# Two attention banks swapped, gh and gl moved into the visit, sines swapped, a third x2t buffer, and the first h of the fixed cycle in a bank of its own

## The chip, the cores and the metric

One core of a Trainium2 chip. The time is device microseconds of one launch, the median of several runs. Five engines run their own instruction queues in order: TensorE (PE), ScalarE (ACT), VectorE (DVE), GpSimd (POOL) and SyncE (SP, which issues the DMAs). PE writes to PSUM, eight banks of 128 x 512 fp32.

## What is computed

A linear attention with a complex decay per key dimension, and behind it two feed-forward layers:

```python
mag = np.sqrt(a_re * a_re + a_im * a_im)
scale = np.minimum(mag, 0.999) / (mag + 1e-06)
a_re_n, a_im_n = a_re * scale, a_im * scale
for t in range(S):                       # B, H, S, D = 4, 8, 768, 48
    new_re = ar * S_re - ai * S_im       # ar, ai: a_re_n, a_im_n at t, per (b, h, d)
    new_im = ar * S_im + ai * S_re
    S_re, S_im = new_re + kv, new_im     # kv = outer(k_t, v_t)
    y[:, :, t] = q_t @ S_re
x = y as 3072 tokens x 384
h = x @ w_in;  x = (h - tanh(h)) @ w_out     # layer 0, d_ff = 2048
h = x @ w_in2; x = relu(h)**2 @ w_out2       # layer 1
```

## The kernel before, in words

*Attention* is cut into 24 units: six chunks of 128 positions (c) for each of four batches (b), unit n = 4c + b. A unit takes logarithms and exponentials of the decay, sums them over positions on PE (pc: sums of the log magnitude; pu: sums of the angle), takes exponentials of pc (ee, in a7x) and two sines of pu's fractional part (fg, in a7 and a8; the last row of F goes by DMA to crow, for the same batch's next chunk), multiplies them into k and q (kn, qn), transposes these (pk, pq), forms masked products of k and q (strips, then wm on DVE), and from these and the state the outputs (px, to xh and xl); pU is the products of kn and v that are added to the state. Chunk 0 is written out in the string START; chunk c = 1 runs as not packed units, chunks 2 to 5 as packed ones.

*Feed-forward.* Six groups g of 512 tokens by 16 blocks m of the hidden width, twice (layers). For a block, g1 forms h in one bank (9 matmuls, because each operand is split into a high and a low float32r part), act_parts turns h into t, gh and gl (ACT: tanh, DVE: subtraction, ACT: the copy gh, DVE: gl = t - gh), and g2 adds to the three accumulators acc (9 matmuls). At a group's end of layer 0, put_x2 copies the three accumulators to tiles x2t (two buffers; ACT, DVE, ACT) and stores them by DMA to DRAM (x2d).

*The order of work.* block_step(t) issues block t's h, the activations of the block before, and the products acc of an older block. NB0 = 17 steps are layer 0's group 0. From t = 17 to 80 (NB0 <= t < NATT) the order is fixed: chain["on"] makes the class Turn issue every instruction of PE, ACT, DVE and SP behind the one traced before it on its engine. Outside of that a planner orders the instructions by its own costs. In the fixed cycle each unit's pieces lie at steps 0 to 15 of its own with a sort key within the step (the list at the end of `unit`: step, key, piece); units follow each other by four steps, so every fourth step is a *visit* (t - NB0 = 3 mod 4), in which one unit does its step 15 (strips, wm, pU, px), the next its 11, the one after that its 7 (a7x), and the next its 3 (a2). Keys below 5 come before the step's h, keys from 5 on after it. In a step, act_step(t, 1) twice does tanh with the subtraction, then gh, for the block just formed; act_step(t - 1, 3) at the next step's start does what is left, gl.

*Banks.* Until t = 17: three accumulators, two banks for h, three for attention. share_banks at t = 17 frees the latter five: two hold the strips (cleared by DVE), and three serve in turn as h, x and y. SHARED tells which of x and y a product uses. `late` is the unit's number past the first packed one; late 0, 1 and 2 straddle the step at t = 17.

*Tables.* ACT holds one table of functions at a time; `table` loads another where the next function isn't in it. tanh is in three of those used, exp and ln share one, sines need `silu_and_others`, arctan `sigmoid_and_others`.

Of the kernel before, what the change touches and what calls it, by code (L numbers as in the profile page):

```python
# [12 lines left out]
F32 = mybir.dt.float32  # L13
# [3 lines left out]
AF = mybir.ActivationFunctionType  # L17
ALU = mybir.AluOpType
AX = mybir.AxisListType
PSUM = bass.MemoryType.PSUM  # L20
# [4 lines left out]
TWO_PI = 6.283185  # L25
# [18 lines left out]
def kernel(  # L44
# [9 lines left out]
    nc = tc.nc  # L54
    B, S, HV, DP = v.shape
    H = HV * 2 // 3
    NG, DM, TG = out.shape
    D = DM // H
    P = 128
# [11 lines left out]
    fctx = ctx.enter_context(ExitStack())  # L71
    spool = fctx.enter_context(tc.tile_pool(name="spool", bufs=2))
    gpool = fctx.enter_context(tc.tile_pool(name="gpool", bufs=2))
# [4 lines left out]
    ps = {  # L78
        "c": ps_c,
        "h": pctx.enter_context(tc.tile_pool(name="ps_h", bufs=2, space=PSUM)),  # L80
        "a": pctx.enter_context(tc.tile_pool(name="ps_a", bufs=3, space=PSUM)),
    }
    SHARED = {"pU": "x", "px": "y", "pc": "x", "pu": "y", "pk": "x", "pq": "y"}
    strips = []

    def ps_tile(tag, name):
        if tag in ps:
            return ps[tag].tile([P, TG], F32, tag=tag, name=name)
        tag = SHARED.get(name, tag if tag in "hxy" else "x")
        return ps["shared"].tile([P, TG], F32, tag=f"s{tag}", name=name, bufs=1)  # L90

    def share_banks():
        pctx.close()
        del ps["h"], ps["a"]
        ps_s = fctx.enter_context(tc.tile_pool(name="ps_s", bufs=1, space=PSUM))
        ps["shared"] = fctx.enter_context(tc.tile_pool(name="ps_x", bufs=1, space=PSUM))
        for i in range(2):
            strips.append(ps_s.tile([P, HH, P], F32, name=f"strips{i}"))
            nc.vector.memset(strips[i], 0.0)

    x2g = [dpool.tile([KD, P, TG], F32, name=f"x2d{g}") for g in range(NG)]

# [9 lines left out]
    for g in range(4):  # L112
        m = maskab[32 * g:32 * g + 32, 1]
# [17 lines left out]
    b_hpi = const.tile([P, 1], F32, name="b_hpi")  # L131
# [5 lines left out]
    chain = {"on": False}  # L137
# [18 lines left out]
    ten, act_e, dve, sp = (Turn(e) for e in (nc.tensor, nc.scalar, nc.vector, nc.sync))  # L156
# [14 lines left out]
    def lut(*a, **kw):  # L171
        if general[0]:
            return act_e.activation(*a, **kw)
        with tc.issue_after(act_set["load"]):
            r = act_e.activation(*a, **kw)
        act_set["ops"].append(r.ins)
        return r
# [7 lines left out]
    n2 = 2 * DM  # L185
# [79 lines left out]
    def g1(layer, m, xt, h, cs=slice(0, TG)):  # L265
        wh, wl = wts[layer, m]
        xh, xl = xt
        n = 3 * KD
        i = 0
        for kk in range(KD):  # L270
            for w_, x_ in ((wh, xh), (wh, xl), (wl, xh)):
                ten.matmul(
                    h, w_[:, kk * P:(kk + 1) * P], x_[:, kk, cs],
                    start=(i == 0), stop=(i == n - 1),
                )
                i += 1
        return h
# [42 lines left out]
    def new_acc():  # L320
        return [ps_c.tile([P, TG], F32, tag="c", name="acc") for _ in range(KD)]

    def put_x2(acc, dst):
        for j in range(KD):
            t = gpool.tile([P, TG], F32, tag="x2t", name="x2t", bufs=2)
            if j % 2 == 0:
                act_e.copy(t, acc[j])
            else:
                dve.tensor_copy(t, acc[j])
            sp.dma_start(dst(j), t)  # L330
# [31 lines left out]
    xts = {}  # L362
# [9 lines left out]
    at = [xpool.tile([P, 2, HH, P], F32, tag=g, name=f"at_{g}") for g in ("xh", "xl")]  # L372
# [16 lines left out]
    def unit(n):  # L389
        c, b = divmod(n, B)  # L390
# [8 lines left out]
        tsl = slice(c * P, (c + 1) * P)  # L399
        HD = H * D  # L400
        V = {}
# [21 lines left out]
        packed = c >= 2  # L423
# [130 lines left out]
        def l3():  # L554
            if early_unit:
                V["vt"] = early("v")
                V["v"] = V["vt"].rearrange("p (h x) -> p h x", h=HV)
            else:
                V["v"] = vz
            sp.dma_start(V["v"], v[b, tsl])  # L560

        def a8():
            F, G = V["F"], V["G"]
            table("trig_and_small" if c == 0 else "silu_and_others")
            V["cs"] = V["ab"] if c == 0 else V["fg"]
            lut(V["cs"][:, :HD], F, AF.Sin, scale=TWO_PI)
            lut(V["cs"][:, HD:], G, AF.Sin, scale=-TWO_PI, bias=b_hpi)

        def a8x():
            dve.tensor_tensor(V["qk"], V["qk"], V["ee"], op=ALU.mult)  # L570
# [194 lines left out]
        if c == 0:  # L765
# [5 lines left out]
                px=a12, x=a12v, pU=a13, st=a13v, ff=fill,  # L771
            )
        def ready(name):
            if chain["on"]:
                table(name)

        if not packed:
# [9 lines left out]
                )  # L787
            ]
        late = n - 2 * B
        return [  # L790
            (0, 5.2, a0), (1, 5.2, a1), (3, 1.4, a2), (3, 1.5, lambda: ready("sigmoid_and_others")),
            (4, 5.1, a3), (5, 5.1, a3b), (6, 6.3 if late < 2 else 1.1, a6l),
            (6, 1.4, a0c), (7, 1.3, a7x), (7, 2.0, l2), (7, 6.1, a4), (7, 7.1, a5c),
            (8, 5.1, a7r), (9, 5.3, a5s), (9, 5.4, a8x),
            (10, 6.3 if late < 1 else 1.1, a6), (10, 6.4 if late < 1 else 1.2, a7),
            (10, 1.3, lambda: ready("silu_and_others")), (10, 6.5, a8),
# [8 lines left out]
    for n in range(B, NU):  # L805
        c, b = divmod(n, B)
# [4 lines left out]
    def attn(s, low=0, high=10):  # L811
        for key, f in sorted(plan.get(s, []), key=lambda x: x[0]):
            if low <= key < high:
                f()
# [170 lines left out]
    def x2_dst(g):  # L985
        return lambda j: x2g[g][j]
# [6 lines left out]
    NB0 = len(blocks)  # L993
# [4 lines left out]
    NB = len(blocks)  # L998
    NATT = NB0 + (NG - 2) * NM
    hs, gs = {}, {}  # L1000
# [8 lines left out]
    def second_half(n):  # L1009
        l, g, m, cs = blocks[n]  # L1010
        if m == 0 and cs.start == 0:
            cur["acc"] = new_acc()
        g2(l, m, gs.pop(n), cur["acc"], cs)
        if m == NM - 1:
            if l == 0:
                put_x2(cur["acc"], x2_dst(g))
            else:
                for j in range(KD):
                    put_out(cur["pool"], cur["acc"], g, j, vector=j % 2 == 1)
# [21 lines left out]
    def act_step(n, parts):  # L1041
        if n not in acts:
            acts[n] = act_parts(
                blocks[n][0], hs.pop(n), cur["pool"], lambda g: gs.__setitem__(n, g),
                third=NB0 <= n < NATT and n % 3 == 2,
            )
        for _ in range(parts):
            next(acts[n], None)

    def block_step(t):  # L1050
        steps = [t - NB0 + NM]
        chain["on"] = NB0 <= t < NATT
        if t < NB0:
            conv_upto(min(NM, blocks[t][2] + JOINS[t]))
            steps = ahead[t]
        if 0 < t <= NB:
            act_step(t - 1, 3)
        if t == NB0:
            share_banks()
        if t < NB:  # L1060
            l, g, m, cs = blocks[t]
            for s in steps[:-1]:
                attn(s)
            for s in steps[-1:]:
                attn(s, 0, 5)
            h = ps_tile("h" if t < NATT else "hxy"[t % 3], "h")[:, :cs.stop - cs.start]
            hs[t] = g1(l, m, xts[l, g], h, cs)
            for s in steps[-1:]:
                attn(s, 5, 6)
                if chain["on"]:  # L1070
                    act_step(t, 1)
                attn(s, 6, 7)
                if chain["on"]:
                    act_step(t, 1)
                attn(s, 7, 10)
        if t == NATT:
            actx.close()
            cur["pool"] = fctx.enter_context(tc.tile_pool(name="ap3", bufs=3))
            cpool[0] = cur["pool"]
        if t == NB:  # L1080
            finish()
            return
        while cur["g2"] < NB and cur["g2"] <= t - (LAG if t >= NATT + 2 else 2):
            second_half(cur["g2"])
            cur["g2"] += 1
        if t == NATT + LAG:
            conv_ahead()
        if t >= NATT + LAG:
            for _ in range(2):
                if cdone[0] < len(cq):  # L1090
                    conv_tick()
            m2 = cur["split"]
            if m2 in joined and t >= NATT + LAG + m2:
                conv_split(1, m2, joined.pop(m2))
                cur["split"] += 1
        if t >= NATT + 2 * NM and t % 2 == 0 and cur["recheck"] < 2 * NM:
            conv_check(*divmod(cur["recheck"], NM))
            cur["recheck"] += 1
        if t >= NATT + 2 * NM and t % 4 == 1 and cur["signs"] < NU // 2:
            sign_check(cur["signs"])  # L1100
            cur["signs"] += 1
        if t < NB and m == NM - 4:
            if l == 1 and g < NG - 1:
                xts[1, g + 1] = get_x2(cur["pool"], x2g[g + 1])
            if l == 0 and g == NG - 1:
                xts[1, 0] = get_x2(cur["pool"], x2g[0])
# [3 lines left out]
    first = {f"{n}{k}": f for n in range(B) for k, f in unit(n).items()}  # L1110
# [103 lines left out]
```

## Time and profile before

| | |
|---|---|
| median of 3 runs | 1036.53 us (1034.96 to 1038.94) |
| the profiled execution | 1038.07 us, of which the span from first to last instruction is 1035.9 |
| busy PE, ACT, DVE | 93%, 62%, 52% of the span |
| mean granted clock of PE | 0.981 of full speed |

All times below are microseconds from the span's start. Matmuls are pipelined: the next begins before the one ahead of it ends, so a row's duration is longer than the distance to the next row. A bracket at a row's end is the idle time of that engine just before it and whose end it waited for. Almost every instruction has the line of one helper (L150), so groups are told apart by the names of their tiles. A group with a count, as x45, is a run of like instructions.

### The profile page before, as it was taken

The numbers are of one execution on the slowest core, as the hardware profiler recorded it, in microseconds if no ns is written. First come the engines' busy times: TensorE is split into PE (matmuls) and PEld (weight loads), VectorE is DVE, ScalarE is ACT, GpSimd is POOL, SyncE is SP. The second block draws the span as 40 slices with busy tenths as digits, with TensorE's granted clock in tenths as the row PEclk, the third lists the DMA queues.
The fourth block names the chain that finished last, engine by engine and source line by source line (L and its number), as shares of the span: only waits on it lengthen the run. The fifth ranks groups of instructions, "written<-read, shape, count | busy, mean of one in ns | idle before, by whom it ended". The sixth has DMA issues, their size and how long they took to land.

```text
span 1035.9 us, 18373 instructions
## 1 busy us (share of the span) xinstructions
PE 965.9 (93%) x7424; PEld 797.5 (77%) x7424; DVE 543.8 (52%) x902; ACT 642.9 (62%) x1132; POOL 19.5 (2%) x41
## 2 busy tenths in 40 slices
PE   3999996998988998999999999999999999999997
PEld 1878775777777776777788887788888888888886
DVE  5899985565555655655654799322232322322211
ACT  8789877677566766776753445546656656555443
POOL 1000000000000000000000001000000000000000
PEclk9999999899989998999999999999999999999999
DMA  6535512222212222212113655005444344341000
GB/s 243 164 131 166 173 44 85 55 55 55 85 54 54 56 75 63 57 55 85 39 55 110 218 180 191 26 18 166 139 136 167 111 148 137 96 147 33 31 1 33
DMA packets 56946, 102.07 MB, mean 99 GB/s; under 512 B 23172, under 2 KB 32664, under 8 KB 56856
## 3 DMA queue, kind: packets, MB, share of 16 engines
q1 hardware_dynamic: 56712, 100.71, 30.5%
q8 instruction: 59, 0.97, 0.4%
q14 instruction: 31, 0.25, 0.1%
q10 hardware_dynamic: 144, 0.13, 0.0%
HBM read 88.14 MB, written 9.47 MB: 94 GB/s over the span
## 4 chain that ended last, share of the span: by engine, by line
PE 72%; ACT 12%; DVE 10%; DMA 4%; issue 1%; SPq 1%; POOL 0%; ACTq 0%; POOLq 0%; DVEq 0%
PE h L150 31%; PE acc L150 28%; PE px L150 4%; ACT L150 3%; DVE jw L150 3%; ACT fg L150 2%; DVE wl L150 2%; PE pU L150 2%; ACT ee L150 2%; DVE gl L150 1%; PE pk L150 1%; PE pq L150 1%; DMA x2d<-x2t 1%; PE strips L150 1%; ACT ab L150 1%; DVE t L150 1%
## 5 line engine op out<-in xcount | busy, mean ns | idle before, releaser
L150 DVE TENSOR_TENSOR gl<-t,gh 128x512 fp32r<-128x512 f32 (+1 forms) x193 | 132.6, 687 | 239.4 <-ACT gh L150 239.4
L150 ACT ACTIVATE t<-h 128x512 f32<-128x512 f32 (+1 forms) x193 | 114.8, 595 | 205.9 <-PE h L150 203.3
L150 PE MATMUL h<-xh,wh 128*128 128x512 f32 (+1 forms) x579 | 228.9, 395 | 8.3 <-DVE t L150 4.9
L150 PE MATMUL acc<-gh,wh 128*128 128x512 f32 (+1 forms) x579 | 228.5, 395 | 2.7 <-ACT x2t L150 2.7
L150 PE MATMUL h<-xl,wh 128*128 128x512 f32 (+1 forms) x579 | 226.0, 390 | 0.3 <-DVE xl L150 0.3
L150 PE MATMUL h<-xh,wl 128*128 128x512 f32 (+1 forms) x579 | 226.3, 391 | 0.0
L150 PE MATMUL acc<-gl,wh 128*128 128x512 f32 (+1 forms) x579 | 225.1, 389 | 0.0
L150 PE MATMUL acc<-gh,wl 128*128 128x512 f32 (+1 forms) x579 | 225.1, 389 | 0.0
L150 ACT CAST gh<-t 128x512 fp32r<-128x512 f32 (+1 forms) x193 | 119.2, 617 | 79.4 <-PE acc L150 38.6
L150 PEld LDWEIGHTS h<-xh,wh 128*128 128x128 f32 x579 | 108.9, 188 | 35.8 <-DVE t L150 7.5
L150 PEld LDWEIGHTS acc<-gh,wh 128*128 128x128 f32 x579 | 108.8, 188 | 24.8 <-ACT x2t L150 3.3
L150 PEld LDWEIGHTS h<-xh,wl 128*128 128x128 f32 x579 | 109.0, 188 | 22.9
L150 PEld LDWEIGHTS acc<-gh,wl 128*128 128x128 f32 x579 | 108.7, 188 | 22.6
L150 PEld LDWEIGHTS h<-xl,wh 128*128 128x128 f32 x579 | 109.0, 188 | 21.6 <-DVE xl L150 0.5
L150 PEld LDWEIGHTS acc<-gl,wh 128*128 128x128 f32 x579 | 108.9, 188 | 21.6 <-DVE gl L150 0.2
L150 DVE TENSOR_TENSOR t<-h,t 128x512 f32<-128x512 f32 (+1 forms) x97 | 66.1, 681 | 65.9 <-ACT t L150 65.8
L150 ACT ACT_TABLE_LOAD x66 | 84.7, 1283 | 1.9 <-PEq L1196 0.8
L150 ACT ACTIVATE t<-t 128x512 f32<-128x512 f32 x96 | 60.3, 628 | 1.7
L150 DVE TENSOR_TENSOR wmin<-wmin,cz 128x768 bf16<-128x768 bf16 x32 | 17.8, 557 | 57.4 <-ACT cz L150 57.4
L150 PE MATMUL pU<-vz,kn 128*32 128x48 f32 x816 | 17.1, 222 | 31.7 <-ACT ee L150 31.7
L150 PEld LDWEIGHTS pU<-vz,kn 128*32 128x32 f32 x816 | 15.1, 121 | 33.3 <-ACT ee L150 33.3
L150 DVE TENSOR_TENSOR wm<-strips,maskab 128x512 f32<-128x512 f32 x32 | 21.7, 689 | 33.2 <-PE strips L150 32.9
(125 smaller groups left out, 1025.7 us busy)
## 6 DMA issues: line engine op xcount, KB each, us to landing
st<-in_w_dram SPq DMA_DIRECT2D x32, 768.0 KB
sr<-in_w_dram SPq DMA_DIRECT2D x32, 768.0 KB
ri<-in_ri_dram SPq DMA_DIRECT2D x24, 384.0 KB
qk<-in_qk_dram SPq DMA_DIRECT2D x24, 384.0 KB
vz<-in_v_dram SPq DMA_DIRECT2D x21, 384.0 KB
x2d<-x2t SPq DMA_DIRECT2D x18, 256.0 KB
xf<-x2d SPq DMA_DIRECT2D x6, 768.0 KB
ss<-in_ri_dram SPq DMA_DIRECT2D x12, 384.0 KB
```

The source lines that it names most:

```text
L150: r = op(*a, **kw)
```

## The change

1. SHARED: pc goes to bank y and pu to bank x.
2. A pool "first" of one bank, made before the strips' pool, gives the h of the steps that ask for the tag "h" after share_banks; the strips and the shared banks lie behind it. The strips are cleared at the end of step 17 and not in share_banks.
3. put_x2 takes its third tile from the pool of the "cv" tiles while the fixed order is on.
4. Units of chunk 1 load 8 of the 12 head blocks that v holds (nv).
5. In packed units the sine with bias (on G) comes before the one on F.
6. For late 2, a2 moves one step earlier, for late 1, a7x one step earlier and a4 with a5c one step later.
7. In the step before a visit gh is no longer issued; in the visit gh follows the keys below 1.35 (the first strips with their mask product, and a7x), and gl follows the keys below 1.75 (a2, pU, the second strips with their mask product).
8. At t = 16 h and the first part of its activation are issued ahead of the attention pieces.

```diff
-    SHARED = {"pU": "x", "px": "y", "pc": "x", "pu": "y", "pk": "x", "pq": "y"}
+    SHARED = {"pU": "x", "px": "y", "pc": "y", "pu": "x", "pk": "x", "pq": "y"}
...
-        return ps["shared"].tile([P, TG], F32, tag=f"s{tag}", name=name, bufs=1)
+        pool = ps["first" if tag == "h" else "shared"]
+        return pool.tile([P, TG], F32, tag=f"s{tag}", name=name, bufs=1)
...
+        ps["first"] = fctx.enter_context(tc.tile_pool(name="ps_f", bufs=1, space=PSUM))
...
-            nc.vector.memset(strips[i], 0.0)
+
+    def clear_strips():
+        for z in strips:
+            dve.memset(z, 0.0)
...
-    def put_x2(acc, dst):
+    def put_x2(acc, dst, third=False):
         for j in range(KD):
-            t = gpool.tile([P, TG], F32, tag="x2t", name="x2t", bufs=2)
+            if third and j == 2:
+                t = spool.tile([P, n2], F32, tag="cv", name="x2t")[:, :TG]
+            else:
+                t = gpool.tile([P, TG], F32, tag="x2t", name="x2t", bufs=2)
...
-            sp.dma_start(V["v"], v[b, tsl])
+            nv = HV if packed else H
+            sp.dma_start(V["v"][:, :nv], v[b, tsl, :nv])
...
-            lut(V["cs"][:, :HD], F, AF.Sin, scale=TWO_PI)
-            lut(V["cs"][:, HD:], G, AF.Sin, scale=-TWO_PI, bias=b_hpi)
+            sins = [
+                lambda: lut(V["cs"][:, :HD], F, AF.Sin, scale=TWO_PI),
+                lambda: lut(V["cs"][:, HD:], G, AF.Sin, scale=-TWO_PI, bias=b_hpi),
+            ]
+            for f in sins[::-1] if packed else sins:
+                f()
...
+        ln = (2, 6.37) if late == 2 else (3, 1.4)
+        ex = (6, 6.36) if late == 1 else (7, 1.3)
+        at = (8, 6.05) if late == 1 else (7, 6.1)
...
-                put_x2(cur["acc"], x2_dst(g))
+                put_x2(cur["acc"], x2_dst(g), third=chain["on"])
...
-        if 0 < t <= NB:
+        visit = NB0 < t < NATT and (t - NB0) % 4 == 3
+        if 0 < t <= NB and not visit:
             act_step(t - 1, 3)
...
+            if t == NB0 - 1:
+                h = ps_tile("h", "h")
+                hs[t] = g1(l, m, xts[l, g], h, cs)
+                act_step(t, 1)
...
-                attn(s, 0, 5)
-            h = ps_tile("h" if t < NATT else "hxy"[t % 3], "h")[:, :cs.stop - cs.start]
-            hs[t] = g1(l, m, xts[l, g], h, cs)
+                attn(s, 0, 1.35)
+                if visit:
+                    act_step(t - 1, 1)
+                attn(s, 1.35, 1.75)
+                if visit:
+                    act_step(t - 1, 1)
+                attn(s, 1.75, 5)
+            if t != NB0 - 1:
+                h = ps_tile("h" if t < NATT else "hxy"[t % 3], "h")[:, :cs.stop - cs.start]
+                hs[t] = g1(l, m, xts[l, g], h, cs)
...
-                if chain["on"]:
+                if chain["on"] and (t - NB0) % 4 != 2:
                     act_step(t, 1)
                 attn(s, 7, 10)
+            if t == NB0:
+                clear_strips()
```

## Rows read from the trace of the kernel before

**Rows 1.** The page: busy time, share of the span and instructions of each engine.

```profile
PE 965.9 (93%) x7424; PEld 797.5 (77%) x7424; DVE 543.8 (52%) x902; ACT 642.9 (62%) x1132; POOL 19.5 (2%) x41
```

**Rows 2.** Sums of waits: who waited for whom, us in total, times, longest.

```profile
PE pU L150 <- ACT ee L150: 31.7, 12, 5.8
...
ACT x2t L150 <- DMA x2d<-x2t: 11.7, 5, 3.0
```

**Rows 3.** Timeline of an ordinary visit: start, duration, engine, operation, [idle before, releaser].

```profile
417.95 0.60 ACT L150 ACTIVATE fg<-fg,b_hpi 128x384 f32<-128x384 f32 x1
...
418.86 0.77 PE L150 MATMUL strips<-kqT 96*32 96x128 f32 x32
419.08 1.28 ACT L150 ACT_TABLE_LOAD   x1
...
420.38 0.87 ACT L150 ACTIVATE ee<-pc 128x384 f32<-128x384 f32 x2
...
421.30 0.84 PE L150 MATMUL pU<-vz,kn 128*32 128x48 f32 x45 [1.67 <-ACT ee L150]
...
422.55 1.06 PE L150 MATMUL px<-kqT,state 96*32 96x128 f32 x32
...
424.42 0.50 PE L150 MATMUL h<-xh,wh 128*128 128x512 f32 x1
...
427.44 0.69 DVE L150 TENSOR_TENSOR t<-h,t 128x512 f32<-128x512 f32 x1 [0.53 <-ACT t L150]
...
428.65 0.39 PE L150 MATMUL h<-xh,wh 128*128 128x512 f32 x1
```

**Rows 4.** Timeline of PE in the four long visits, the second of them whole.

```profile
183.62 1.42 PE L150 MATMUL pU<-vz,kn 128*32 128x48 f32 x45 [4.56 <-ACT ee L150]
...
282.17 0.77 PE L150 MATMUL strips<-kqT 96*32 96x128 f32 x32
288.75 1.42 PE L150 MATMUL pU<-vz,kn 128*32 128x48 f32 x45 [5.81 <-ACT ee L150]
...
294.25 0.50 PE L150 MATMUL h<-xh,wh 128*128 128x512 f32 x1
...
317.16 1.03 PE L150 MATMUL pU<-vz,kn 128*32 128x48 f32 x45 [3.50 <-ACT ee L150]
...
394.86 1.42 PE L150 MATMUL pU<-vz,kn 128*32 128x48 f32 x45 [4.98 <-ACT ee L150]
```

**Rows 5.** Windows: busy us by engine, then granted PEclk, DMA share, GB/s.

```profile
284.00:298.00 14.00, 9.25 (x160) 8.41 (x161) 6.26 (x13) 8.42 (x16) 0.00 (x0) 0.76 0.13 31
564.00:578.00 14.00, 14.00 (x63) 11.60 (x62) 8.10 (x11) 5.10 (x10) 2.21 (x3) 1.00 0.88 301
```

**Rows 6.** Timeline of ACT and of SP's queue (SPq) ahead of three long visits.

```profile
280.38 0.59 ACT L150 COPY x2t<-acc 128x512 f32<-128x512 f32 x1 [2.71 <-DMA x2d<-x2t]
...
309.74 0.57 SPq L150 DMA_DIRECT2D crow<-fg  x1
...
313.38 0.52 ACT L150 ACTIVATE fg<-fg 128x384 f32<-128x384 f32 x1 [1.83 <-DMA crow<-fg]
...
389.27 0.57 SPq L150 DMA_DIRECT2D crow<-fg  x1
...
391.09 0.52 ACT L150 ACTIVATE fg<-fg 128x384 f32<-128x384 f32 x1 [0.52 <-DMA crow<-fg]
```

**Rows 7.** Timeline of PE and ACT at the step that opens the cycle.

```profile
158.95 0.47 PE L150 MATMUL h<-xh,wh 128*128 128x512 f32 x1 [3.03 <-DVE state L150]
...
163.90 0.59 ACT L150 ACTIVATE t<-h 128x512 f32<-128x512 f32 x1
...
166.88 0.50 PE L150 MATMUL h<-xh,wh 128*128 128x512 f32 x1 [2.85 <-DVE t L150]
...
170.00 0.63 PE L150 MATMUL h<-xh,wl 128*128 128x512 f32 x1
```

**Rows 8.** Timeline of PE in the first visit of the last chunk.

```profile
495.42 1.45 PE L150 MATMUL px<-wm,vz 128*32 128x128 f32 x32 [1.79 <-DVE wm L150]
```

More of the change, by code (lines that the diff above doesn't have):

```diff
@@ L789, in unit @@
         late = n - 2 * B
+        ln = (2, 6.37) if late == 2 else (3, 1.4)
+        ex = (6, 6.36) if late == 1 else (7, 1.3)
+        at = (8, 6.05) if late == 1 else (7, 6.1)
         return [
-            (0, 5.2, a0), (1, 5.2, a1), (3, 1.4, a2), (3, 1.5, lambda: ready("sigmoid_and_others")),
+            (0, 5.2, a0), (1, 5.2, a1), ln + (a2,), (3, 1.5, lambda: ready("sigmoid_and_others")),
             (4, 5.1, a3), (5, 5.1, a3b), (6, 6.3 if late < 2 else 1.1, a6l),
-            (6, 1.4, a0c), (7, 1.3, a7x), (7, 2.0, l2), (7, 6.1, a4), (7, 7.1, a5c),
+            (6, 1.4, a0c), ex + (a7x,), (7, 2.0, l2), at + (a4,), (at[0], 7.1, a5c),
             (8, 5.1, a7r), (9, 5.3, a5s), (9, 5.4, a8x),
```

## The prediction

> **What bounds the kernel now.** I read the page first, then the sums of waits, then TensorE (PE), ScalarE (ACT), VectorE (DVE) and the SyncE queue (SP) in order of time, around each visit of the fixed cycle and around the step that opens it. PE is busy 93% of the span [rows 1], so a change can only pay where PE still stands idle or runs at its lower clock. The sums say where: twelve times, 31.7 us together, PE waits before the pU products for ACT's exponentials `ee` [rows 2]. ACT itself loses 11.7 us in five waits for an x2t buffer [rows 2].
>
> An ordinary visit shows why [rows 3]. The strips products start at 418.86. pU lies in bank x, and so does pc, from which ACT takes two exponentials. ACT runs sines, gh, table load, exponentials in that order; the exponentials end at 420.38 + 0.87 = 421.25, and pU starts at 421.30, after 1.67 us of idle PE. From strips to the visit's h are 424.42 - 418.86 = 5.56 us, so 3.89 without the wait.
>
> Twelve visits have this wait: eight ordinary ones and four long ones with 4.56, 5.81, 3.50 and 4.98 us, 18.85 together [rows 4]; the eight share 31.7 - 18.85 = 12.85, or 1.6 each. A long wait costs twice: after 5.81 us of idle the pU group took 1.42 us against 0.84, as the granted clock of 284 to 298, 0.76 on average, had part of it at 1.2 GHz and not 2.4 [rows 5], and from strips to h are 294.25 - 282.17 = 12.08 us: 3.89 of work, 5.81 of wait, 2.38 lost to the clock. Three of the long ones follow a group's end, where ACT stood 2.71 us before its second x2t copy; the fourth, at 317, follows a sine that stood 1.83 us for the crow transfer [rows 6].
>
> **The change part by part.** The sum is made on the profiled execution, 1038.07 us (span 1035.9 and 2.2 around it), 1.5 above the median of 1036.53.
>
> *pc and pu swap banks; gh and gl into the visit; ordinary visits.* pU then shares x with pu, whose readers are done a step earlier; px shares y with pc. PE: strips end at 421.30 - 1.67 = 419.63, pU starts at once, px follows 422.55 - 421.30 = 1.25 later, at 420.88, which is 2.02 after the strips' start. ACT: the sines end at 417.95 + 0.60 = 418.55; without gh there the load starts at once, so the exponentials end 1.28 + 0.02 + 0.87 = 2.17 later, at 420.72. px arrives about 0.1 after them. The 1.6 us go, and next in line is px behind the same exponentials with only that cover. I take 0.15 of new wait per visit, 1.45 gained, eight times 11.6; the bounds are 1.6 and 1.0 (exponentials 0.5 to 0.6 late, about the length of one sine). gh now stands on ACT between exponentials and logarithms, gl on DVE behind both mask products; their readers, the next step's acc products, come after that step's h. Behind them on DVE wait kn, qn, state, xl and the visit's subtraction, which frees the h bank: it ended at 428.13, the next h started at 428.65 [rows 3]. With PE 1.67 and DVE about 1.6 earlier that half microsecond stays; if it went, each visit would lose what is missing. No instruction is added.
>
> *Third x2t buffer, sines swapped; the four long visits.* With a buffer of its own the second ACT copy follows the first as soon as the accumulator is full, and 2.7 us of ACT's lateness go. The sine that reads G no longer stands behind the crow transfer, which reads F; the other one still does. What a crow transfer takes, from issue to the sine that waited for it, is 1.82 us in one place and 3.64 in another [rows 6]. For the visit at 282 I get: copy done 280.38 - 2.71 + 0.6 = 278.2, pu's reader and F, each 0.6 later, so crow issued 279.4, landed 281.2 to 283.0; sines done 281.8 to 283.5; exponentials 2.17 later, 284.0 to 285.7. px is ready at 282.17 + 2.02 = 284.19. It waits 0 to 1.5; I take 0.7, and 0.7 and 0.4 for its two sisters. At 317 the long transfer stays and the swap hides one sine of 0.5 and gh's move 0.6: sine 313.38 to 313.90, exponentials 316.07, px ready 314.91, wait 1.2. So the four keep 3.0 (bounds 1.2 to 5.7) of 18.85 + 8.4, where 8.4 is 2.38 for the clock at the first and 2.0 each for the others, an estimate by their pU rows (1.42, 1.42, 1.03 against 0.84). Gain 27.25 - 3.0 = 24.2.
>
> The three x2d stores now go out closer together, with crow behind them on SP's queue. The rows don't show that order mattering: crow took 1.82 us at a group's end (389.27) and 3.64 within a group (309.74) [rows 6]. The Trainium skill (DMA: Bandwidth & Descriptors, "Queues, rings and completion order") says that descriptors are consumed in ring order on each DMA engine, so crow would start behind the third store's 256 KB. By that rule the three waits lie at their upper ends, 2.5 us in all against my sum.
>
> The table load's price matters more: the load at 419.08 took 1.28 us, and the exponential began 0.02 after it [rows 3]. The Trainium skill (ScalarE: Activation LUTs, "What ACT_TABLE_LOAD costs") adds a drain of about 1.38 us to each switch. By it px would wait 1.3 us more in each of the 14 visits that have exponentials, some 18 us in all; the rows leave no room for such a drain.
>
> *Last chunk.* Its visits have no pU. At 495 px waited 1.79 us for a mask product [rows 8], held behind gl and gh after a late x2t copy: now about 0.65, gain 1.1. The next visit loses 0.5, since px comes there pU's 0.64 us sooner and meets the exponentials. The last two have none. Together 0.6.
>
> *h in an idle bank, and the three moved pieces.* At 158.95 the first h of the cycle starts after 3.03 us, behind state's read of the pU that lay in its bank [rows 7]. In the new bank it can start at 155.9. 18 products take 428.65 - 424.42 = 4.2 us [rows 3], transposes about 0.6: the second h could start at 160.7 and not at 166.88. What holds it is ACT: before the tanh at 163.90 lie sines, a table load, exponentials, logarithms, a second load, an arctangent and another tanh [rows 7]. The change puts the earlier tanh, exponentials and logarithms ahead of the sines, the arctangent and its load behind this tanh; that takes about 2.4 us (1.28 + 0.53 + 0.58) from in front of it, the subtraction and kn, qn still to come: second h at about 162.9, 4.0 gained. The eight starts from 166.88 to 170.00 took 3.12 us where 8 x 0.235 = 1.9 is usual, so 1.2 of lower clock go too. I take 5.2, bounds 0 (sines and so kn and qn now late) and 7.4. The er transfer goes out a step earlier, ahead of its reader; the strips are cleared a step's end later, three steps before their use.
>
> *v load.* A third less for the units before chunk 2. No PE wait above 1 us in those steps is on it: 0, at most 0.5.
>
> Sum: 11.6 + 24.2 + 0.6 + 5.2 = 41.6 us. 1038.07 - 41.6 = 996.5; on the median 1036.53 - 41.6 = 995. Bounds: 12.85 + 26.0 + 1.1 + 7.4 = 47 at the top (989), 8 + 21.5 + 0 + 0 = 29.5 at the bottom (1007). After the cycle nothing absorbs this: from 564 on PE is busy 14.00 of 14 us at full clock [rows 5], so a shift there shifts the end.
>
> **The rivals.**
> 1. The wait moves to px. For it: both stand behind the same exponentials, and the cover is 0.1 us. Against: px comes 1.25 us later than pU did, and gh leaves ACT ahead of them. With 1 us of wait in the 14 visits the gain is 41.6 - 12 = 30: 1007.
> 2. The opening step gains nothing, or loses 3 us. For it: outside the cycle the planner orders the instructions, and sines, kn and qn now stand behind more table work. Against: ACT had idle time there. 1000 to 1003.
> 3. The clock and the long waits stay: the x2t wait wasn't what made ACT late, or crow lands late again. Then the three visits keep 4 us each: 1007.
> 4. Slower: ACT becomes the loop's bound. px waits for exponentials, xh for px, the next tanh for xh, and the next exponentials for all of it. It decides from where the exponentials end 41.6 / 14 = 3.0 us later than worked out, about 4.9 after the strips' start; at 4 us later the time is 1036.5 + 14 = 1051. Against: in the cycle's other steps ACT stands waiting for h, so lateness doesn't add up.
> 5. The swap does nothing, because the planner's tile release still ties pU to an earlier reader: only x2t and sines (about 2.7 us of wait and 1 of clock in three visits), the last chunk and the opening step gain, 17 us: 1020.
>
> **How the numbers follow.** Chances: forecast 0.64, rival 1 0.12, rival 2 0.10, rival 3 0.05, rival 4 0.04, rival 5 0.05. Forecast 995; its own range 988 to 1001; with rivals 1 to 3 the range is 985 to 1010, leaving out rivals 4 and 5 and a little at both ends. A change within 0.5% (5 us) can't be told from none here. Faster than that: 0.94, the forecast and rivals 1, 2, 3 and 5 but for the outer 0.02 of their tails; within: 0.02; slower: 0.04, rival 4.
>
> **What would show it.** Right: no wait of pU for `ee`; px after strips by 2.0 to 2.3 us in ordinary visits; the way from strips to h under 4.2 us where it was 5.56; no x2t wait inside the cycle; the granted clock at full in the long visits; no wait of the first h for state. Wrong: a px wait for `ee` above 0.5 us in most visits, waits of h for the subtraction, or pk waiting for kn in the opening step.

## The result, and the profile after

The changed kernel takes 998.63 us, the median of four runs (995.56 to 1000.25); the kernel before took 1035.74 on the same chip. The ratio is 0.9636 [0.96, 0.9672]: 3.6% faster, with 995 forecast. The profiled execution is the fastest of the four, 995.56 (span 993.6, clock 0.996), against 1038.07 (span 1035.9, clock 0.981); the sum gave 996.5 for it. So the spans differ by 42.3 us and the medians by 37.1.

The page's line of busy time, after. PE is busy 12.8 us less with the same 7424 products [rows 1], as fewer of them run at the lower clock: px of the fifth visit takes 1.92 us in experiment 3, behind a long wait, and 1.08 here.

```profile
PE 953.1 (96%) x7424; PEld 786.6 (79%) x7424; DVE 543.4 (55%) x902; ACT 643.6 (65%) x1133; POOL 19.3 (2%) x41
```

The sums of waits, after: us in total, times, longest. The 31.7 us of pU behind `ee` [rows 2] are gone as a line; px waits for `ee` in six places, 4.5 us together (0.97, 0.87, 1.01 and 0.69 in the four long visits, 0.47 in each of two visits of the last chunk).

```profile
PE px L155 <- ACT ee L155: 4.5, 6, 1.0
PE pu L155 <- ACT kqT L155: 2.6, 1, 2.6
PE acc L155 <- ACT x2t L155: 2.5, 1, 2.5
...
ACT fg L155 <- DMA crow<-fg: 4.7, 5, 1.1
ACT x2t L155 <- DMA x2d<-x2t: 3.8, 2, 2.6
```

An ordinary visit after, PE and then ACT (start, duration, engine, line, operation). It answers to [rows 3].

```profile
383.48 0.77 PE L155 MATMUL strips<-kqT 96*32 96x128 f32 x32
384.06 0.81 PE L155 MATMUL pU<-vz,kn 128*32 128x48 f32 x45
...
385.30 1.06 PE L155 MATMUL px<-kqT,state 96*32 96x128 f32 x32
...
387.17 0.50 PE L155 MATMUL h<-xh,wh 128*128 128x512 f32 x1
```

```profile
382.04 0.61 ACT L155 ACTIVATE fg<-fg,b_hpi 128x384 f32<-128x384 f32 x1
382.55 0.51 ACT L155 ACTIVATE fg<-fg 128x384 f32<-128x384 f32 x1
383.07 1.28 ACT L155 ACT_TABLE_LOAD   x1
384.36 0.87 ACT L155 ACTIVATE ee<-pc 128x384 f32<-128x384 f32 x2
385.12 0.62 ACT L155 CAST gh<-t 128x512 fp32r<-128x512 f32 x1
```

No PE row has a bracket: no idle time. Strips to h is 387.17 - 383.48 = 3.69 us, where it was 5.56. The exponentials end at 384.36 + 0.87 = 385.23 and px, 1.24 behind pU, starts at 385.30: the cover of 0.1 us that the prediction worked out is about 0.07 here, and it holds. gh follows the exponentials on ACT.

The long visit that answers to the one at 282 [rows 4], PE, then ACT and SP's queue (SPq):

```profile
268.47 0.77 PE L155 MATMUL strips<-kqT 96*32 96x128 f32 x32
...
271.33 1.08 PE L155 MATMUL px<-kqT,state 96*32 96x128 f32 x32 [0.87 <-ACT ee L155]
...
273.22 0.50 PE L155 MATMUL h<-xh,wh 128*128 128x512 f32 x1
```

```profile
263.39 1.07 ACT L155 COPY x2t<-acc 128x512 f32<-128x512 f32 x2
...
268.57 0.52 ACT L155 ACTIVATE fg<-fg 128x384 f32<-128x384 f32 x1 [0.94 <-DMA crow<-fg]
...
270.41 0.87 ACT L155 ACTIVATE ee<-pc 128x384 f32<-128x384 f32 x2
```

```profile
266.14 0.57 SPq L155 DMA_DIRECT2D crow<-fg  x1
```

Both x2t copies now run as one group (x2) with nothing ahead of the second; what is left is the sine behind the crow transfer, and 0.87 us of px. Strips to h is 4.75 us where it was 12.08.

The step that opens the cycle [rows 7], PE, then ACT and SP's queue:

```profile
153.30 0.88 PE L155 MATMUL pU<-vz,kn 128*32 128x48 f32 x48
...
155.33 0.49 PE L155 MATMUL h<-xh,wh 128*128 128x512 f32 x1 [1.15 <-ACT xh L155]
...
161.64 0.39 PE L155 MATMUL h<-xh,wh 128*128 128x512 f32 x1
...
169.19 0.69 PE L155 MATMUL pu<-th,tri 128*128 128x384 f32 x1 [2.63 <-ACT kqT L155]
...
175.79 0.77 PE L155 MATMUL strips<-kqT 96*32 96x128 f32 x32
```

```profile
167.03 0.84 ACT L155 ACTIVATE ab<-ri 128x768 f32<-128x768 f32 x1 [4.70 <-DMA ri<-in_ri_dram]
```

```profile
162.87 0.43 SPq L155 DMA_DIRECT2D ri<-in_ri_dram  x1
```

The second h stands at 161.64 and not at 166.88. ACT then waits 4.70 us, until 167.03, for the load of `ri`, which SP issues only at 162.87, and PE waits 2.63 us for the kqT copies that stand behind it on ACT.

Windows of the long visit and of that place: length, busy us by engine (PE, PEld, DVE, ACT, POOL), granted clock, DMA share, GB/s. The long visit has the full 2.4 GHz (0.76 before [rows 5]); behind the ri wait part of the time is at 1.2.

```profile
268.00:282.00 14.00, 13.13 (x220) 10.97 (x219) 9.27 (x17) 10.81 (x20) 0.00 (x0) 1.00 0.31 88
169.00:176.00 7.00, 6.81 (x33) 5.42 (x37) 4.31 (x7) 4.98 (x9) 0.00 (x0) 0.76 0.38 128
```

**Where the 42.2 us came from**, from the start of the strips in the sixteenth visit, 558.13 before and 515.97 after; from there to the end it is 477.8 and 477.6 us. Strips to h is summed over the visits of a kind.

| part | before | after | gained | worked out |
|---|---|---|---|---|
| eight ordinary visits | 46.12 | 31.57 | 14.55 | 11.6 |
| four long visits | 42.71 | 19.06 | 23.65 | 24.2 |
| last chunk, its two visits with exponentials | 8.39 | 7.39 | 1.0 | 0.6 |
| opening step, pU of unit 7 to the first strips | 23.26 | 22.49 | 0.8 | 5.2 |
| up to that pU (start of it) | 155.03 | 153.30 | 1.7 | 0 |
| between visits, the rest | | | 0.5 | 0 |

### The profile page after: what moved, and what is told of

It is laid out like the page before. It is cut to its first block, busy times and chain, and to the rows that moved or that the text cites. A ratio compares the mean times of both kernels' runs of the same rounds, so it can differ in the third digit from the quotient of the medians.

```text
span 993.6 us, 18356 instructions
## 1 busy us (share of the span) xinstructions
PE 953.1 (96%) x7424; PEld 786.6 (79%) x7424; DVE 543.4 (55%) x902; ACT 643.6 (65%) x1133; POOL 19.3 (2%) x41
## 4 chain that ended last, share of the span: by engine, by line
PE 71%; ACT 10%; issue 7%; DVE 7%; DMA 4%; SPq 1%; POOL 0%; ACTq 0%; POOLq 0%; DVEq 0%
PE h L155 31%; PE acc L155 30%; PE px L155 4%; ACT L155 3%; ACT ab L155 2%; DMA crow<-fg 1%; PE strips L155 1%; ACT ee L155 1%; PE pk L155 1%; ACT fg L155 1%; PE pq L155 1%; DMA ri<-in_ri_dram 1%; DVE cv L155 1%; PE pU L155 1%; ACT gh L155 1%
## 5 line engine op out<-in xcount | busy, mean ns | idle before, releaser
L155 ACT ACTIVATE ab<-ri 128x768 f32<-128x768 f32 x24 | 20.3, 848 | 17.7 <-DVE ll L155 9.8
L155 DVE SCALAR_TENSOR_TENSOR jw<-st,jw 128x768 int32<-128x768 int32 x32 | 30.4, 951 | 0.2
```

The lines of the kernel that those rows point to most:

```text
L155: r = op(*a, **kw)
```

## The experiments

Each was timed in five rounds beside the kernel before. Experiments 8 to 11 ran on one chip and the other experiments on another; the ratio is to the kernel before on the same chip, so where two chips are compared the ratios count. A diff is against the changed kernel, except where it says before.

**1. Banks swapped back.**

```
-    SHARED = {"pU": "x", "px": "y", "pc": "y", "pu": "x", ...}
+    SHARED = {"pU": "x", "px": "y", "pc": "x", "pu": "y", ...}
```

> The changed kernel with pc and pu back in their old banks, all else kept. Theory: the bank swap is what lets pU pass the exponentials; without it pU waits again, by about 1.3 us in the eight ordinary visits (exponentials end 1.9 us after the strips start, pU is ready at 0.6) and 2.2 in the four with a late sine, less the px waits of 3.5 us that it replaces: +16 us, about 1014. Rival: moving gh off ACT ahead of the exponentials was what took the wait away; then no pU wait over 0.5 us and 999.

Measured: 1013.32 us, ratio 0.9766 [0.9744, 0.9788]. The wait is back in twelve visits (sums of waits, then PE's timeline in the ninth, the longest): 1.03 us in each ordinary one, 1.96 to 2.16 in the long ones. Strips to h in an ordinary visit is 4.92 us against 3.69. That it was the shared bank that held pU behind the exponentials is shown; the swap is worth some 14 us with the other edits in place (by the ratios, 13.5 against the first timing of the changed kernel and 14.7 against experiment 8).

```profile
PE pU L155 <- ACT ee L155: 16.4, 12, 2.2
```

```profile
374.21 0.84 PE L155 MATMUL pU<-vz,kn 128*32 128x48 f32 x45 [2.16 <-ACT ee L155]
```

**2. gh and gl back in the chain's step.**

```
-        visit = NB0 < t < NATT and (t - NB0) % 4 == 3
+        visit = False
...
-                if chain["on"] and (t - NB0) % 4 != 2:
+                if chain["on"]:
```

> The changed kernel with gh and gl back at the end of the step before the visit and the visit's start. Theory: the cover of px is 0 to 0.1 us, so gh's 0.62 us ahead of the table load shows as a px wait of about 0.5 us in each of 14 visits: +7 us, about 1006. Rival: ACT has slack there and px waits for its mask product anyway: 999.

Measured: 1004.03 us, 0.9689 [0.9669, 0.9709]. All fourteen visits with exponentials have px waiting; an ordinary one of the later ones takes 4.21 us. So it is gh's and gl's move that keeps the thin cover. The sums, and one visit's px:

```profile
PE px L155 <- ACT ee L155: 9.1, 14, 1.3
```

```profile
387.31 1.08 PE L155 MATMUL px<-kqT,state 96*32 96x128 f32 x32 [0.33 <-ACT ee L155]
```

**3. No third x2t buffer.**

```
-                put_x2(cur["acc"], x2_dst(g), third=chain["on"])
+                put_x2(cur["acc"], x2_dst(g), third=False)
```

> The changed kernel with two x2t buffers as before. Theory: ACT is 2.5 us late again in the three visits after a group's end, px waits that much longer and PE's clock falls there: +8 to +11 us, about 1008. Rival: with pU no longer behind ACT and gh moved, most of the lateness is covered: under +3 us, 1001.

Measured: 1011.24 us, 0.9738 [0.9718, 0.9758], 12.6 above the changed kernel's 998.63, or 10.6 to 11.8 by the ratios: at the upper end of the 8 to 11 expected or over it. Four visits suffer and not three: the first, fifth, ninth and thirteenth take 6.05, 9.02, 7.57 and 7.89 us, where the changed kernel has 4.86, 4.75, 4.57 and 3.70. In the fifth, ACT and then PE:

```profile
268.61 0.59 ACT L155 COPY x2t<-acc 128x512 f32<-128x512 f32 x1 [2.71 <-DMA x2d<-x2t]
...
274.95 0.87 ACT L155 ACTIVATE ee<-pc 128x384 f32<-128x384 f32 x2
```

```profile
270.40 0.77 PE L155 MATMUL strips<-kqT 96*32 96x128 f32 x32
...
275.87 1.92 PE L155 MATMUL px<-kqT,state 96*32 96x128 f32 x32 [3.48 <-ACT ee L155]
```

The wait of 2.71 us is as long as that of [rows 6]. It moves through ACT's queue to px, and the px group then takes 1.92 us instead of 1.08.

**4. The swap alone, on the kernel before.**

```
-    SHARED = {"pU": "x", "px": "y", "pc": "x", "pu": "y", ...}
+    SHARED = {"pU": "x", "px": "y", "pc": "y", "pu": "x", ...}
```

> The kernel before with the bank swap alone. Theory: pU's wait goes, px waits for the exponentials that still stand behind gh, 0.55 us in ordinary visits; gain about 1.1 us in each of eight, 1.3 and about 1 of clock in each of four: -18 us, about 1018. Rival: the swap alone brings nearly all that the visits gained (-31): about 1005; other rival: it brings nothing, the wait moving to px whole: 1035.

Measured: 1024.93 us, 0.9878 [0.9859, 0.9896]: 13 us and not 18. The twelve visits with pU are not where it falls short. The eight ordinary ones take 4.2 to 4.3 us and gain 11.8 together. The long ones keep 7.83, 10.88, 6.16 and 8.27 us, their wait now before px, and gain 9.6, about what was expected. What the expectation left out is the rest. The first two visits of the last chunk, which had no pU to wait, now wait with px and take 7.56 and 4.21 us where they took 5.38 and 3.01; the ways between visits are 2.9 us longer in all; and from the sixteenth strips to the end it takes 480.3 us and not 477.8.

```profile
PE px L150 <- ACT ee L150: 22.4, 14, 5.3
```

**5. h of the opening step back in its old bank, the moved pieces kept.**

```
-        pool = ps["first" if tag == "h" else "shared"]
+        pool = ps["shared"]
...
-        ps["first"] = fctx.enter_context(...)
```

> The changed kernel with the first h of the cycle back in a bank that the attention used. Theory as predicted: h waits for state's read of pU again, 3.0 us; behind it ri's landing hides most, so 0 to +2 at the end, 999. Rival: with the moved pieces DVE does state right behind pU, 154.8, and h waits for xh until 155.3 anyway, so the bank is worth nothing here: no wait on state, 998.3.

Measured: 996.05 us, 0.9593 [0.9567, 0.9619], not slower than with the bank. The first h waits for its own operand `xl` and not for state; DVE reads pU for state at 153.70, as soon as pU is done. So with the moved pieces the bank is worth nothing that can be measured. PE, then DVE:

```profile
152.76 0.88 PE L154 MATMUL pU<-vz,kn 128*32 128x48 f32 x48
...
155.41 0.47 PE L154 MATMUL h<-xh,wh 128*128 128x512 f32 x1 [1.76 <-DVE xl L154]
```

```profile
153.70 0.55 DVE L154 TENSOR_TENSOR state<-state,pU 96x384 f32<-96x384 f32 x1 [0.44 <-PE pU L154]
```

**6. The moved pieces back, the bank kept.**

```
-        ln = (2, 6.37) if late == 2 else (3, 1.4)
+        ln = (3, 1.4)
...
-            if t == NB0 - 1:
+            if False:
...
```

(and `ex` and `at` in the same way, and the h of that step issued behind the attention work again.)

> The changed kernel with the opening step as before: a2, a7x and a4 at their old steps, h and its activation of step 16 not ahead of the attention pieces; the bank of h kept. Theory: the second h is late again by some 3 us, as the tanh ahead of it stands behind tables once more; but the changed kernel waits for ri a step later until about 167, so only 0 to 2 us of it reach the first visit: 998 to 1000. Rival: the moves are worth their whole 4 us: 1003.

Measured: 1000.16 us, 0.9639 [0.9614, 0.9664]; the interval holds the changed kernel's 0.9636. The second h of the cycle comes at 167.74 again, but no ri wait follows, and the strips start at 177.43. The first h of the cycle now waits longest of all, 7.47 us, and by its bracket for DVE's `t`, a subtraction that reads an earlier h, where the kernel before had 3.03 us for state [rows 7]. So the new bank by itself does not let the first h start early; it only exchanges one reader for another. From unit 7's pU, at 152.40 here, to the first strips it takes 25.03 us, more than the 23.26 of the kernel before.

```profile
160.75 0.79 PE L155 MATMUL h<-xh,wh 128*128 128x512 f32 x1 [7.47 <-DVE t L155]
```

**7. The whole v load again.**

```
-            nv = HV if packed else H
+            nv = HV
```

> The changed kernel with v loaded whole in the units before chunk 2. Theory: the 1.7 us by which pU of unit 7 starts sooner (155.0 before, 153.3 after) isn't the smaller load, as no PE wait there names it: 998.3. Rival: the 128 KB less per unit bring the queue's later loads forward: +1.5, 1000.

Measured: 998.89 us, 0.9623 [0.9597, 0.965], no difference. Its profiled execution, the slowest it had, has unit 7's pU 2.6 us later than the changed kernel's. The other profiles say the same: with the whole load that pU starts at 155.03 (before), 155.12 (experiment 4) and 155.88 (here), and in all eleven profiles with the smaller load at 152.40 to 154.53. So the 1.7 us in the table point to the smaller load, although the time of the kernel shows nothing of it; where it is lost again was not looked for.

```profile
155.88 0.88 PE L155 MATMUL pU<-vz,kn 128*32 128x48 f32 x48
```

**8. The changed kernel once more, unchanged.**

> The changed kernel again, on the same chip as the next three: 998.6 by its earlier median, 995.6 to 1000.3. If the visits with a px wait for the exponentials (1, 5, 6 and 9 of 16 in its first profile) are others this time, they are the visits where a crow transfer happened to be late; if they are the same, their place in the schedule makes them.

Measured: 998.22 us, 0.9624 [0.9596, 0.9651]. The px waits stand in the same visits, the four long ones and two of the last chunk, so they belong to the order of the work. What differs most between the two profiles is the change of layers at 607: there acc waits 3.48 us for an x2t copy, against 2.55 in the first profile, and PE's granted clock is 0.61 in that stretch where it was 1.00. From the sixteenth strips to the end it took 481.0 us, not 477.6. The changed kernel's timeline and window, then those of this run:

```profile
607.30 0.50 PE L155 MATMUL acc<-gh,wh 128*128 128x512 f32 x1 [2.55 <-ACT x2t L155]
```

```profile
606.00:612.00 6.00, 4.70 (x21) 3.89 (x22) 5.42 (x7) 3.66 (x7) 0.00 (x0) 1.00 0.15 58
```

```profile
608.67 0.80 PE L155 MATMUL acc<-gh,wh 128*128 128x512 f32 x1 [3.48 <-ACT x2t L155]
```

```profile
606.00:612.00 6.00, 3.33 (x8) 2.66 (x9) 4.22 (x6) 3.45 (x6) 0.00 (x0) 0.61 0.28 107
```

**9. F in a tile of its own**, so that no sine overwrites what the crow transfer still reads.

```
             if c > 0:
                 pair("fg", "F", "G")
+            if packed:
+                t1("F", F32)
```

> The changed kernel with F in a tile of its own in the packed units, so that the sine on F no longer overwrites what the crow transfer reads and waits for nothing. Theory: the px waits left over (0.7 to 1.0 us in four visits, 3.5 together) are crow's; without them -3.5 us, 995, and the px distance is 1.83 in all twelve visits with pU. Rival: ACT is late there by its own work; then the waits stay and the time is 998.6.

Measured: 992.9 us, 0.9566 [0.9536, 0.9595], 5.3 below experiment 8. ACT has no crow wait any more, and px comes 1.82 to 1.83 us behind the strips in every visit with pU but the first. The fifth, ACT and then PE:

```profile
266.88 0.51 ACT L155 ACTIVATE fg<-F 128x384 f32<-128x384 f32 x1
```

```profile
267.81 0.77 PE L155 MATMUL strips<-kqT 96*32 96x128 f32 x32
...
269.63 1.07 PE L155 MATMUL px<-kqT,state 96*32 96x128 f32 x32
```

The px waits alone were worked out at 3.5. The other part lies in the opening step, where the ri wait is gone as well: SP issues that load at 161.52 and no longer at 162.87, and ACT, which comes to it later, waits by its bracket for DVE instead. From unit 7's pU to the first strips it takes 20.53 us, against 22.91 in experiment 8. SP's queue, then ACT:

```profile
161.52 0.43 SPq L155 DMA_DIRECT2D ri<-in_ri_dram  x1
```

```profile
166.66 0.85 ACT L155 ACTIVATE ab<-ri 128x768 f32<-128x768 f32 x1 [1.11 <-DVE ll L155]
```

**10. Unit 11's ri load issued a step earlier.**

```
-            (0, 5.2, a0), ...
+            ((-1, 1.0) if late == 3 else (0, 5.2)) + (a0,), ...
```

> The changed kernel with unit 11's load of ri one step earlier, ahead of the opening step. Theory: the opening step gained only 0.8 us where 5.2 were worked out because, shorter, it meets that load: ACT's square waits 4.7 us for it, PE 2.6, and PE's clock falls behind it; without it -4 us, 994.6, and visit 1 starts about 13.5 us after the first h and not 20. Rival: something behind it on ACT or DVE is as late (qn, the table loads), so that under 1 us comes back: 998.

Measured: 997.2 us, 0.9615 [0.9588, 0.9643]: mostly the rival. The ri wait goes and the first strips start at 171.65, 4.1 us sooner; but now the exponentials of the first visit are late, px waits and runs at the lower clock, and h comes at 179.07, 7.42 after the strips instead of 4.86. 1.6 of the 4.1 us are left in the profiles; the medians, 1.0 us below experiment 8's with intervals that overlap, can't be told apart. ACT, then PE:

```profile
172.80 0.52 ACT L155 ACTIVATE fg<-fg 128x384 f32<-128x384 f32 x1 [0.99 <-DMA crow<-fg]
...
174.63 0.87 ACT L155 ACTIVATE ee<-pc 128x384 f32<-128x384 f32 x2
```

```profile
171.65 0.77 PE L155 MATMUL strips<-kqT 96*32 96x128 f32 x32
...
175.56 1.94 PE L155 MATMUL px<-kqT,state 96*32 96x128 f32 x32 [1.92 <-ACT ee L155]
```

**11. Experiments 9 and 10 together.** Both diffs above.

> Both edits together. Theory: they add, -7.5 us, about 991. Rival: each uncovers the other's successor, -4 us: 994.5.

Measured: 993.39 us, 0.958 [0.9548, 0.9612], no better than 9 alone. The rows of experiment 9 say why: there the ri wait is gone already, and from unit 7's pU to the first strips it takes 20.44 us here against 20.53 there.

**12. Both, and the third x2t buffer in every group**, so at the change of layers too.

```
-                put_x2(cur["acc"], x2_dst(g), third=chain["on"])
+                put_x2(cur["acc"], x2_dst(g), third=True)
```

> ri earlier, F in a tile of its own, and the third x2t buffer also outside the fixed order. Theory: the one x2t wait left, at the change of layers, costs PE 2.5 to 4.0 us and in some executions 1.5 to 4 more of lower clock behind it, which is most of the scatter between executions; without it about 988.5, executions within 3 us of each other. Rival: there the next wait (x of layer 1, or the weights on DVE) ends as late: 993, scatter as before.

Measured: 987.53 us, 0.952 [0.9493, 0.9546], the fastest of all kernels here, 11 us below the changed one and 5.9 below experiment 11 (6.2 by the ratios). The acc wait is gone, PE is busy without a gap there at full clock (window below), and the executions lie within 2.6 us of each other.

```profile
596.00:611.00 15.00, 15.00 (x68) 12.43 (x67) 8.64 (x12) 8.49 (x14) 0.00 (x0) 1.00 0.37 139
```

The swap of the sines was not undone by itself; experiment 9 takes away what it was for.

## Why the prediction was right, step by step

- *Ordinary visits* (11.6; measured 14.55). The mechanism is the one worked out, and experiments 1 and 2 show both halves of it. In the visit at 383 the size was low on two terms. The 0.15 us of new px wait didn't come: rival 1, with px behind the exponentials everywhere, is what experiment 2 gives, in a smaller size. And pU starts 384.06 - 383.48 = 0.58 after the strips and not 0.77, since a group that waits for nothing starts before the modelled end of the one ahead; a bracket of 1.67 us was worth 5.56 - 3.69 = 1.87. So px comes 1.82 us behind the strips, a little under the 2.0 to 2.3 that were to show the prediction right. But the eight are not alike, as the working took them to be. The last five gained 9.0 of the 14.55. The third visit kept 4.51 us and gained only 0.94; the fourth kept 4.47, and both stay over the 4.2 us named as a sign. The fourth still gained 2.72, as before it took 7.19 us: its 1.65 us of wait was followed by lower clock (the kernel before, window below), and that came back too. The working costed lower clock in the long visits alone.

```profile
256.00:264.00 8.00, 6.35 (x180) 5.70 (x179) 4.75 (x9) 6.11 (x11) 0.00 (x0) 0.79 0.02 4
```

- *Long visits* (24.2; 23.65). The waits left are 0.97, 0.87, 1.01 and 0.69, together 3.5, for 3.0 worked out. The crow transfer of the fifth visit is issued at 266.14 and its sine starts at 268.57: 2.43 us, between the two ends of [rows 6]. The three visits behind a group's end keep 0.97, 0.87 and 0.69, together 2.5 us, where the prediction's sum has 1.8. The clock's share came back in full, and experiment 3 shows the way from the x2t buffer to it. The ring-order rule of the Trainium skill (DMA: Bandwidth & Descriptors, "Queues, rings and completion order"), as the prediction used it, put these three waits at their upper ends. By that estimate 2.5 us come on top of the 1.8 and the fifth visit keeps 1.5; 0.7 on top of the 1.8 and 0.87 were measured. No run here changes the order on the queue, so the rule itself was not tested.
- *Table load.* The load of 383.07 takes 1.28 us and the exponential follows 0.01 later. The Trainium skill (ScalarE: Activation LUTs, "What ACT_TABLE_LOAD costs") adds a drain of about 1.38 us to each switch of tables. No such time stands in these rows, before the load or behind it.
- *Opening step* (5.2; 0.8). This step failed, in two ways. From unit 7's pU to the second h it takes 161.64 - 153.30 = 8.34 us where it took 166.88 - 155.03 = 11.85, so 3.5 of the 4.0 us worked out did come, and the nine products of that h run at full speed (8 starts in 1.82 us). But the shortened step ran into unit 11's ri load: ACT 4.70 us, PE 2.63, and lower clock behind it; from the second h to the first strips it takes 14.15 us where it was 11.41. The working never asked when that load is issued and what frees its buffer. Experiment 10 shows the load as the cause, and the first visit's exponentials as next late. And the bank was costed as what lets the first h start at 155.9; it isn't idle. Experiment 6 shows that without the moved pieces h waits there 7.47 us for another reader, and experiment 5 that with them the bank is worth nothing, as that h then waits for its own operand.
- *Last chunk* (0.6; 1.0). The wait for the mask product went, and px waits 0.47 us for the exponentials in each of the two visits. *v load* (0, at most 0.5): none seen in the time of experiment 7, but 1.7 us up to unit 7's pU point to it.

So the total was met partly by luck, because misses cancel: 3.0 us too little for the ordinary visits and 1.7 us that the sum put at nothing, against 4.4 too much for the opening step. The profile flatters the sum besides. The two profiled executions lie 42.5 us apart against the 41.6 worked out, but the one after is the fastest of its four; the medians lie 37.1 apart, 4.5 us short. Rivals 3, 4 and 5 are excluded by the rows; rival 2 happened in the size of its step, without moving the sum out of the forecast's own range.

## What to carry to other kernels

Choose which products share a bank by when their readers finish: a product that could start early must not stand with one whose reader ends last. When a wait is removed, list what comes next on every queue of the shortened stretch, loads and what frees their buffers included; a step made shorter earns only up to the next late thing. An operation that overwrites in place a tile which a transfer reads makes its engine wait for that transfer; a tile of its own cost no busy time here and gave 5.3 us, about 2.4 of them in the opening step.

## What the runs showed of the hardware

- A short idle time of PE can cost more than itself: behind 2.63 us (at 169.19) the granted clock of the next 7 us was 0.76, and at 607 an idle of 3.48 us was followed by 1.2 GHz for part of the time where 2.55 us kept it at 1.00 in another execution of the same kernel. Nor does the length alone decide: 1.65 us at 258.69 in the kernel before was followed by a granted clock of 0.79 over the window of 256 to 264, while behind 1.67 us at 421.30 px took its usual 1.06 us [rows 3]. Experiment 12 has no such idle there and its executions lie within 2.6 us; those of experiment 9, with 4.0 us of it in its profile, lie within 6.7, but those of experiment 8 within 1.7. That this place makes most of the scatter is likely and was not shown.
- The same small transfer of one row, crow, took 1.82 and 3.64 us from issue to its waiting reader at two places of the cycle before, and 2.43 at a place of the cycle after.
